# Running a decoder layer's projections and feed-forward per half of the batch, and pooling the K and V buffers, in a two-layer attention kernel

## The chip, the cores and the metric

The kernel runs on one core of a Trainium2 chip. The metric is the time of one execution on the device in microseconds (us), as the median of several runs. A run counts as slow when it is over 1.5% above the fastest run of the same kernel, else as fast. Ratios are the mean of one kernel's fast runs over the mean of the other's fast runs of the same rounds, with a 95% interval, so they are not quite the ratios of the medians.

## The reference, cut to what matters

```python
B, Sq, D = 4, 1, 512                    # four sequences, one new token each
Hq, Hkv, Sk, Dh = 32, 8, 4096, 128      # GQA: 4 query heads per kv head
F = 1792
# A: q = norm(x) @ wq; softmax(q k^T / sqrt(Dh)) v; @ wo     (k and v: caches, bf16)
# B: (gelu(norm(x) @ w_gate) * (norm(x) @ w_up)) @ w_down
x = x + A(x); x = x + B(x)              # layer 1
x = x + A(x); x = x + B(x)              # layer 2, the same caches and weights
```

There are 32 pairs (batch, kv head). Each has 1 MiB of K and 1 MiB of V, which both layers read: 128 MiB, plus 13.25 MiB of weights, 148 MB in all.

## The kernel before

A layer first works through all 32 pairs' scores, then through all 32 pairs' outputs; projections and the feed-forward part (FFN) follow. Abridged:

```python
K_BUFS = 3; V_BUFS = 3                       # K_j and V_j tiles of 1 MiB
...
for j in range(NPAIR):                       # scores
    K_j = issue_k(j)                         # DMA
    # 32 transposes on TensorE, copied from PSUM to KT_j by VectorE and ScalarE
    # 32 matmuls: sc = KT_j . q
    nc.scalar.activation(out=SCORES[:, j], in_=sc, func=ACT.Copy)
    nc.vector.tensor_reduce(out=colmax, in_=sc, op=ALU.max)            # 3 buffers
    nc.gpsimd.partition_all_reduce(gmax, colmax, P, RED.max)           # 3 buffers
    nc.gpsimd.tensor_scalar(out=NEGB[:, j], in0=gmax, scalar1=-scale, op0=ALU.mult)
for j in range(NPAIR):                       # outputs
    V_j = ...                                # DMA
    # 4 x pexp = exp(scale * SCORES + NEGB), with SUMS, on ScalarE      (4 buffers)
    nc.gpsimd.partition_all_reduce(den, SUMS[:, j], P, RED.add)
    # 32 matmuls: ot += V_j . pexp           (2 PSUM buffers)
    nc.vector.tensor_tensor(out=OT_bf[:, b, qsl], in0=ot, in1=1/den, op=ALU.mult)
# out-proj (128 matmuls), layer norm, FFN (3 x 56), layer norm, next q-proj (128)
```

A scheduler places the instructions of the two loops on each engine ahead of time, so the first outputs are woven into the last scores. PSUM is where the kernel puts the tiles that TensorE writes (tp, sc, ot); a denominator is the sum that a softmax divides by.

Of the kernel before, what the change touches and what calls it, by code (L numbers as in the profile page):

```python
# [15 lines left out]
P = 128  # L16

K_BUFS = 3
KT_BUFS = 3
V_BUFS = 3  # L20
# [8 lines left out]
def kernel(  # L29
# [27 lines left out]
    KB = KD * B  # L57
    assert Hq * B <= P and B <= P and rep <= P and KB <= 512
    assert C * rep * 4 <= 2048, "scores tile must fit a PSUM bank"
    assert 2 * KF * B * 4 <= 2048 and rep * B <= C * rep  # L60
# [11 lines left out]
    kin = ctx.enter_context(tc.tile_pool(name="kin", bufs=K_BUFS))  # L72
    ktp = ctx.enter_context(tc.tile_pool(name="ktp", bufs=KT_BUFS))
    vin = ctx.enter_context(tc.tile_pool(name="vin", bufs=V_BUFS))
# [38 lines left out]
    H_bf = state.tile([P, KF, B], BF16, name="H_bf")  # L113
# [4 lines left out]
    def layer_norm_T():  # L118
        xs = small.tile([P, 2, KD, B], FP32, name="xs", tag="xs")
        nc.vector.tensor_tensor(out=xs[:, 1], in0=XT[:], in1=XT[:], op=ALU.mult)  # L120
        st = ps_misc.tile([P, 2, KD, B], FP32, name="st", tag="misc")
        nc.tensor.matmul(st[:, 0], lhsT=ones_f[:, :], rhs=XT[:, :, :], start=True, stop=True)
        nc.tensor.matmul(st[:, 1], lhsT=ones_f[:, :], rhs=xs[:, 1], start=True, stop=True)
        sums = small.tile([P, 2, B], FP32, name="sums", tag="sums")
        nc.vector.tensor_reduce(out=sums[:], in_=st.rearrange("p s k b -> p s b k"),
                                axis=AX.X, op=ALU.add)
        negmean = small.tile([P, B], FP32, name="negmean", tag="negmean")
        nc.vector.tensor_scalar(out=negmean[:, :], in0=sums[:, 0, :], scalar1=-1.0 / D,
                                scalar2=None, op0=ALU.mult)
        msq = small.tile([P, B], FP32, name="msq", tag="msq")  # L130
        nc.vector.tensor_tensor(out=msq[:, :], in0=negmean[:, :], in1=negmean[:, :],
                                op=ALU.mult)
        var = small.tile([P, B], FP32, name="var", tag="var")
# [3 lines left out]
        hv = small.tile([P, B], I32, name="hv", tag="hv")  # L137
        nc.vector.tensor_single_scalar(out=hv[:, :], in_=var[:, :].bitcast(I32), scalar=1,
                                       op=ALU.arith_shift_right)
        rstd = small.tile([P, B], FP32, name="rstd", tag="rstd")  # L140
        nc.vector.tensor_tensor(out=rstd[:, :].bitcast(I32), in0=magic[:, :], in1=hv[:, :],
                                op=ALU.subtract)
        r2 = small.tile([P, B], FP32, name="r2", tag="r2")
        for _it in range(2):
# [5 lines left out]
        xc = small.tile([P, KD, B], FP32, name="xc", tag="xc")  # L150
        nc.vector.tensor_tensor(out=xc[:], in0=XT[:],
                                in1=negmean[:, :].unsqueeze(1).broadcast_to([P, KD, B]),
                                op=ALU.add)
        nc.vector.tensor_tensor(out=xnT_bf[:], in0=xc[:],  # L154
                                in1=rstd[:, :].unsqueeze(1).broadcast_to([P, KD, B]),
                                op=ALU.mult)

    def add_yT_to_XT(yT_ps):
        nc.vector.tensor_tensor(out=XT[:], in0=XT[:], in1=yT_ps[:], op=ALU.add)
# [11 lines left out]
    def issue_k(j):  # L171
        b, kvh = divmod(j, Hkv)
        K_j = kin.tile([P, C, Dh], BF16, name="K_j", tag="K_j")
        dq.dma_start(out=K_j[:], in_=A_k_cache[b, kvh].rearrange("(p c) d -> p c d", p=P))
        return K_j

    layer_idx = [0]

    def attention_layer():
        first = layer_idx[0] == 0  # L180
        layer_idx[0] += 1
        pre_k = {}
        if first:
            npre = min(K_BUFS, NPAIR)
# [5 lines left out]
        layer_norm_T()  # L190
        for kvh in range(Hkv):
            qps = ps_sc.tile([P, rep, B], FP32, name="qps", tag="sc")
            for h in range(rep):
                m = kvh * rep + h
                for k in range(KD):
                    nc.tensor.matmul(qps[:, h, :], lhsT=wq_sb[:, k, m * Dh:(m + 1) * Dh],  # L196
                                     rhs=xnT_bf[:, k, :], start=(k == 0), stop=(k == KD - 1))
            nc.vector.tensor_copy(out=qT_bf[:, kvh * rep:(kvh + 1) * rep, :], in_=qps[:, :, :])
# [28 lines left out]
        for j in range(NPAIR):  # L227
# [5 lines left out]
            V_j = vin.tile([P, C, Dh], BF16, name="V_j", tag="V_j")  # L233
# [11 lines left out]
            for c in range(C):  # L245
# [3 lines left out]
                                    op=ALU.mult)  # L249

        yT = ps_misc.tile([P, KD, B], FP32, name="yT", tag="misc")
        for dk in range(KD):
            for i in range(Hq):
                nc.tensor.matmul(yT[:, dk, :], lhsT=wo_sb[:, i, dk * P:(dk + 1) * P],  # L254
                                 rhs=OT_bf[:, :, i], start=(i == 0), stop=(i == Hq - 1))
        add_yT_to_XT(yT)

    def ffn_layer():
        layer_norm_T()
        NF = KF * B  # L260
        hg = ps_misc.tile([P, KF, B], FP32, name="hg", tag="misc")
        for m in range(KF):
            for k in range(KD):
                nc.tensor.matmul(hg[:, m, :], lhsT=wg_sb[:, k, m * P:(m + 1) * P],  # L264
                                 rhs=xnT_bf[:, k, :], start=(k == 0), stop=(k == KD - 1))
        g_sb = small.tile([P, NF], FP32, name="g_sb", tag="g_sb")
        nc.vector.tensor_copy(out=g_sb[:, :], in_=hg.rearrange("p m b -> p (m b)"))
        t1 = small.tile([P, NF], FP32, name="t1", tag="t1")
        nc.vector.tensor_tensor(out=t1[:, :], in0=g_sb[:, :], in1=g_sb[:, :], op=ALU.mult)
# [9 lines left out]
        for m in range(KF):  # L279
            for k in range(KD):  # L280
                nc.tensor.matmul(hu[:, m, :], lhsT=wu_sb[:, k, m * P:(m + 1) * P],
                                 rhs=xnT_bf[:, k, :], start=(k == 0), stop=(k == KD - 1))
# [52 lines left out]
```

## Time and profile before

The median was 592.04 us in the first six runs. The profiled run was a slow one. I cut it into stages at marks that the GpSimd and TensorE timelines show: the first max all-reduce; the first all-reduce after the last negation of the layer (from there only V is left); the last 100 matmuls of the out-projection; the first scores of layer 2.

| us | start | layer-1 scores | layer-1 V tail | chain to layer 2 | layer-2 scores | layer-2 V tail | end | span |
|---|---|---|---|---|---|---|---|---|
| before, first profile (slow) | 27.7 | 226.9 | 52.0 | 25.7 | 233.0 | 17.7 | 16.2 | 599.2 |
| before, second profile | 27.3 | 222.2 | 51.1 | 24.8 | 233.9 | 18.2 | 16.2 | 593.7 |

In the profiles PE is TensorE's matmuls, PEld its weight loads, DVE VectorE, ACT ScalarE, POOL GpSimd, and SPq the queue that issues the DMAs. Two rows of slices from the page of the kernel before (40 equal slices of the span, busy tenths), then from its groups of instructions (line, engine, operation, tiles, count; busy us and mean ns of one; idle us just before and what ended it):

```profile
POOL 0001201101010111031100012021101110211100
...
DMA  8968792866496571779977485745675584963560
...
L211 PE MATMUL tp<-ident_bf,K_j 128*128 128x128 bf16 x2048 | 170.3, 254 | 13.9 <-ACT KT_j L169 6.9
...
L223 POOL PARTITION_ALL_REDUCE gmax<-colmax x64 | 23.9, 428 | 225.0 <-issue 153.4
...
L224 POOL TENSOR_SCALAR NEGB<-gmax 128x4 f32<-128x4 f32 x64 | 15.1, 235 | 191.5 <-DVE KT_j L167 115.5
```

GpSimd is busy for 66.4 of 599.2 us (11%), yet its two small operations have 225 and 192 us of idle time before them, and the larger part of the first is "issue": nothing that the profile shows was waited for. The DMA row has two full slices in a row only where V is left alone (270 to 300 us).

### The profile page before, as it was taken

To read this page: it belongs to the slowest core of one execution; us is meant where nothing else is said; L and a number is where in the kernel's file an instruction comes from. 1 tells how busy PE (TensorE), PEld (TensorE's weight loads), DVE (VectorE), ACT (ScalarE), POOL (GpSimd) and SP (SyncE) were. 2 spreads that over 40 slices of the span, in tenths; PEclk is the share of its full clock that TensorE was granted. 3 is DMA by queue.
4 is the path that set the end of the run, shared out by engine and by line. 5 is a ranking of instruction groups with operands and counts; after the bars stand their busy time and mean duration, and the time that the engine had idled before them with its cause. 6 is when DMAs were issued, how large, how long until landed. Compare 5 with 4: busy or idle time off the path is not lost. (4 is left out here: it accounts for less than half of the span.)

```text
span 599.2 us, 16150 instructions
## 1 busy us (share of the span) xinstructions
PE 307.9 (51%) x7016; PEld 295.4 (49%) x7016; DVE 181.8 (30%) x495; ACT 170.9 (29%) x643; POOL 66.4 (11%) x198
## 2 busy tenths in 40 slices
PE   1996834756334410163467993573466436411145
PEld 1986824656334410153466983573466436411144
DVE  2555512534223100031125571442244223100103
ACT  0245411322113430265300244431332225431210
POOL 0001201101010111031100012021101110211100
PEclk9979865887676555565556696865876676555555
DMA  8968792866496571779977485745675584963560
GB/s 334 364 222 288 261 378 97 311 250 256 177 369 232 209 275 80 280 301 378 368 293 276 152 341 220 274 165 207 270 260 209 181 337 159 362 225 114 203 278 2
DMA packets 26551, 149.16 MB, mean 249 GB/s; under 512 B 2152, under 2 KB 8048, under 8 KB 10096
## 3 DMA queue, kind: packets, MB, share of 16 engines
q1 hardware_dynamic: 26480, 148.13, 66.1%
q8 instruction: 55, 0.90, 0.6%
q14 instruction: 16, 0.13, 0.1%
HBM read 148.12 MB, written 0.00 MB: 247 GB/s over the span
## 5 line engine op out<-in xcount | busy, mean ns | idle before, releaser
L211 PE MATMUL tp<-ident_bf,K_j 128*128 128x128 bf16 x2048 | 170.3, 254 | 13.9 <-ACT KT_j L169 6.9
L211 PEld LDWEIGHTS <-K_j 128*128 128x128 bf16 x2048 | 154.0, 116 | 18.6 <-issue 10.8
L167 DVE COPY KT_j<-tp 128x1024 bf16<-128x1024 bf16 x192 | 129.2, 688 | 68.0 <-PE tp L211 60.5
L246 PE MATMUL ot<-pexp,V_j 128*128 128x4 bf16 x2048 | 61.4, 166 | 128.1 <-DVE OT_bf L248 78.8
L216 PE MATMUL sc<-qT_bf,KT_j 128*128 128x4 bf16 x2048 | 63.5, 166 | 121.4 <-DVE colmax L220 120.6
L216 PEld LDWEIGHTS <-KT_j 128*128 128x128 bf16 x2048 | 63.1, 103 | 124.2 <-issue 122.7
L246 PEld LDWEIGHTS <-V_j 128*128 128x128 bf16 x2048 | 58.2, 102 | 131.0 <-issue 82.4
L237 ACT ACTIVATE pexp<-SCORES,NEGB 128x32 bf16<-128x32 f32 x256 | 86.7, 355 | 108.1 <-PE ot L246 101.2
L169 ACT ACTIVATE KT_j<-tp 128x1024 bf16<-128x1024 bf16 x64 | 65.4, 1021 | 108.9 <-PE tp L211 107.3
L218 ACT ACTIVATE SCORES<-sc 128x128 f32<-128x128 f32 x64 | 17.8, 279 | 183.8 <-PE sc L216 183.8
L220 DVE TENSOR_REDUCE colmax<-sc 128x4 f32<-128x128 f32 x64 | 18.4, 289 | 144.5 <-POOL gmax L223 136.1
L223 POOL PARTITION_ALL_REDUCE gmax<-colmax x64 | 23.9, 428 | 225.0 <-issue 153.4
L237 ACT ACTIVATION_READ_ACCUMULATOR pexp<-SCORES,NEGB 128x1 f32 x256 | 48.0, 188 | 0.0
L243 DVE RECIPROCAL rden<-den 128x4 f32<-128x4 f32 x64 | 11.3, 177 | 105.0 <-POOL den L241 102.8
L241 POOL PARTITION_ALL_REDUCE den<-SUMS x64 | 28.5, 481 | 80.7 <-issue 44.1
L224 POOL TENSOR_SCALAR NEGB<-gmax 128x4 f32<-128x4 f32 x64 | 15.1, 235 | 191.5 <-DVE KT_j L167 115.5
L248 DVE TENSOR_TENSOR OT_bf<-ot,rden 128x4 bf16<-128x4 f32 x64 | 10.0, 160 | 63.8 <-PE ot L246 63.2
L196 PEld LDWEIGHTS <-wq_sb 128*128 128x128 bf16 x256 | 7.6, 103 | 6.5 <-issue 6.5
L254 PEld LDWEIGHTS <-wo_sb 128*128 128x128 bf16 x256 | 8.8, 103 | 3.8 <-issue 3.8
L196 PE MATMUL qps<-xnT_bf,wq_sb 128*128 128x4 bf16 x256 | 7.3, 166 | 6.2 <-DVE xnT_bf L154 6.2
L254 PE MATMUL yT<-OT_bf,wo_sb 128*128 128x4 bf16 x256 | 8.8, 168 | 3.0 <-DVE OT_bf L248 3.0
L274 ACT ACTIVATE th<-t_9168 128x56 f32<-128x56 f32 x1 | 0.2, 249 | 20.6 <-DVE t_9168 L272 20.6
(68 smaller groups left out, 51.6 us busy)
## 6 DMA issues: line engine op xcount, KB each, us to landing
K_j<-in_A_k_cache_dram SPq DMA_DIRECT2D x64, 1024.0 KB, 5.7
V_j<-in_A_v_cache_dram SPq DMA_DIRECT2D x64, 1024.0 KB, 7.6
wq_sb<-in_A_wq_dram SPq DMA_DIRECT2D x2, 2048.0 KB, 13.7
wo_sb<-in_A_wo_dram SPq DMA_DIRECT2D x1, 4096.0 KB, 17.9
wg_sb<-in_B_w_gate_dram SPq DMA_DIRECT2D x1, 1792.0 KB
wu_sb<-in_B_w_up_dram SPq DMA_DIRECT2D x1, 1792.0 KB, 10.7
wd_sb<-in_B_w_down_dram SPq DMA_DIRECT2D x1, 1792.0 KB, 10.6
x_bf<-in_A_x_dram SPq DMA_DIRECT2D x1, 4.0 KB
```

Source lines behind the costliest of these rows:

```text
L167: nc.vector.tensor_copy(out=out_ap, in_=in_ap)
L169: nc.scalar.activation(out=out_ap, in_=in_ap, func=ACT.Copy)
L211: nc.tensor.transpose(tp[:, t, :], K_j[:, c, :], ident_bf[:, :])
L216: nc.tensor.matmul(sc[:, c, :], lhsT=KT_j[:, c, :], rhs=qcols, start=True, stop=True)
L218: nc.scalar.activation(out=SCORES[:, j, :, :], in_=sc[:, :, :], func=ACT.Copy)
L220: nc.vector.tensor_reduce(out=colmax[:, :], in_=sc.rearrange("p c h -> p h c"), axis=AX.X, op=ALU.max)
L223: nc.gpsimd.partition_all_reduce(gmax[:, :], colmax[:, :], P, RED.max)
L224: nc.gpsimd.tensor_scalar(out=NEGB[:, j, :], in0=gmax[:, :], scalar1=-scale, scalar2=None, op0=ALU.mult)
L237: nc.scalar.activation(out=pexp[:, :, h], in_=SCORES[:, j, :, h], func=ACT.Exp, bias=NEGB[:, j, h:h + 1], scale=scale, accum_out=SUMS[:, j ...
L241: nc.gpsimd.partition_all_reduce(den[:, :], SUMS[:, j, :], P, RED.add)
L246: nc.tensor.matmul(ot[:, :], lhsT=V_j[:, c, :], rhs=pexp[:, c, :], start=(c == 0), stop=(c == C - 1))
L254: nc.tensor.matmul(yT[:, dk, :], lhsT=wo_sb[:, i, dk * P:(dk + 1) * P], rhs=OT_bf[:, :, i], start=(i == 0), stop=(i == Hq - 1))
```

## The change

The intent was to take layer 1's projections and FFN off the boundary between the layers: once half of the batch has its attention outputs, its out-projection, FFN and layer-2 q-projection run while V of the other half still streams. In the same edit the three K and three V buffers became one pool of six. The diff, cut to its core:

```diff
-K_BUFS = 3
-V_BUFS = 3
+KV_BUFS = 6
...
-        K_j = kin.tile([P, C, Dh], BF16, name="K_j", tag="K_j")
+        K_j = kvin.tile([P, C, Dh], BF16, name="K_j", tag="kv")
...
-            V_j = vin.tile([P, C, Dh], BF16, name="V_j", tag="V_j")
+            V_j = kvin.tile([P, C, Dh], BF16, name="V_j", tag="kv")
...   (layer_norm_T, q_proj, out_proj_add and ffn now take a range b0, nb of the batch)
+            if kvh == Hkv - 1:
+                after_batch(b)
...
+    NBH = (B + 1) // 2
+    def after_batch_l1(b):
+        if b + 1 == NBH or b + 1 == B:
+            b0 = 0 if b + 1 == NBH else NBH
+            nb = b + 1 - b0
+            out_proj_add(b0, nb)
+            ffn(b0, nb)
+            layer_norm_T(b0, nb)
+            q_proj(b0, nb)
```

Layer 2 still does everything for the whole batch at its end.

More of the change, by code (lines that the diff above doesn't have):

```diff
@@ L56 @@
     NPAIR = B * Hkv
-    KB = KD * B
-    assert Hq * B <= P and B <= P and rep <= P and KB <= 512
+    assert Hq * B <= P and B <= P and rep <= P and KD * B <= 256
     assert C * rep * 4 <= 2048, "scores tile must fit a PSUM bank"
-    assert 2 * KF * B * 4 <= 2048 and rep * B <= C * rep
+    assert KF * 4 <= 2048 and 2 * KD * B * 4 <= 2048
     scale = float(Dh) ** -0.5
@@ L71 @@
     pexpp = ctx.enter_context(tc.tile_pool(name="pexpp", bufs=PEXP_BUFS))
-    kin = ctx.enter_context(tc.tile_pool(name="kin", bufs=K_BUFS))
+    kvin = ctx.enter_context(tc.tile_pool(name="kvin", bufs=KV_BUFS))
     ktp = ctx.enter_context(tc.tile_pool(name="ktp", bufs=KT_BUFS))
-    vin = ctx.enter_context(tc.tile_pool(name="vin", bufs=V_BUFS))
     ps_tp = ctx.enter_context(tc.tile_pool(name="ps_tp", bufs=TP_PSUM_BUFS, space=bass.MemoryType.PSUM))
@@ L112 @@
     xnT_bf = state.tile([P, KD, B], BF16, name="xnT_bf")
-    H_bf = state.tile([P, KF, B], BF16, name="H_bf")
     SCORES = state.tile([P, NPAIR, C, rep], FP32, name="SCORES")
@@ L116, with layer_norm_T @@
     SUMS = state.tile([P, NPAIR, rep], FP32, name="SUMS")
-    def layer_norm_T():
-        xs = small.tile([P, 2, KD, B], FP32, name="xs", tag="xs")
-        nc.vector.tensor_tensor(out=xs[:, 1], in0=XT[:], in1=XT[:], op=ALU.mult)
-        st = ps_misc.tile([P, 2, KD, B], FP32, name="st", tag="misc")
-        nc.tensor.matmul(st[:, 0], lhsT=ones_f[:, :], rhs=XT[:, :, :], start=True, stop=True)
-        nc.tensor.matmul(st[:, 1], lhsT=ones_f[:, :], rhs=xs[:, 1], start=True, stop=True)
-        sums = small.tile([P, 2, B], FP32, name="sums", tag="sums")
+    def layer_norm_T(b0, nb):
+        bs = slice(b0, b0 + nb)
+        xs = small.tile([P, KD, nb], FP32, name="xs", tag=f"xs{nb}")
+        nc.vector.tensor_tensor(out=xs[:], in0=XT[:, :, bs], in1=XT[:, :, bs], op=ALU.mult)
+        st = ps_misc.tile([P, 2, KD, nb], FP32, name="st", tag="misc")
+        nc.tensor.matmul(st[:, 0], lhsT=ones_f[:, :], rhs=XT[:, :, bs], start=True, stop=True)
+        nc.tensor.matmul(st[:, 1], lhsT=ones_f[:, :], rhs=xs[:], start=True, stop=True)
+        sums = small.tile([P, 2, nb], FP32, name="sums", tag=f"sums{nb}")
         nc.vector.tensor_reduce(out=sums[:], in_=st.rearrange("p s k b -> p s b k"),
                                 axis=AX.X, op=ALU.add)
-        negmean = small.tile([P, B], FP32, name="negmean", tag="negmean")
+        negmean = small.tile([P, nb], FP32, name="negmean", tag=f"negmean{nb}")
         nc.vector.tensor_scalar(out=negmean[:, :], in0=sums[:, 0, :], scalar1=-1.0 / D,
                                 scalar2=None, op0=ALU.mult)
-        msq = small.tile([P, B], FP32, name="msq", tag="msq")
+        msq = small.tile([P, nb], FP32, name="msq", tag=f"msq{nb}")
         nc.vector.tensor_tensor(out=msq[:, :], in0=negmean[:, :], in1=negmean[:, :],
                                 op=ALU.mult)
-        var = small.tile([P, B], FP32, name="var", tag="var")
+        var = small.tile([P, nb], FP32, name="var", tag=f"var{nb}")
         nc.vector.tensor_scalar(out=var[:, :], in0=sums[:, 1, :], scalar1=1.0 / D,
@@ L136, in layer_norm_T @@
         nc.vector.tensor_tensor(out=var[:, :], in0=var[:, :], in1=msq[:, :], op=ALU.subtract)
-        hv = small.tile([P, B], I32, name="hv", tag="hv")
+        hv = small.tile([P, nb], I32, name="hv", tag=f"hv{nb}")
         nc.vector.tensor_single_scalar(out=hv[:, :], in_=var[:, :].bitcast(I32), scalar=1,
                                        op=ALU.arith_shift_right)
-        rstd = small.tile([P, B], FP32, name="rstd", tag="rstd")
-        nc.vector.tensor_tensor(out=rstd[:, :].bitcast(I32), in0=magic[:, :], in1=hv[:, :],
+        rstd = small.tile([P, nb], FP32, name="rstd", tag=f"rstd{nb}")
+        nc.vector.tensor_tensor(out=rstd[:, :].bitcast(I32), in0=magic[:, :nb], in1=hv[:, :],
                                 op=ALU.subtract)
-        r2 = small.tile([P, B], FP32, name="r2", tag="r2")
+        r2 = small.tile([P, nb], FP32, name="r2", tag=f"r2{nb}")
         for _it in range(2):
@@ L149, in layer_norm_T @@
             nc.vector.tensor_tensor(out=rstd[:, :], in0=rstd[:, :], in1=r2[:, :], op=ALU.mult)
-        xc = small.tile([P, KD, B], FP32, name="xc", tag="xc")
-        nc.vector.tensor_tensor(out=xc[:], in0=XT[:],
-                                in1=negmean[:, :].unsqueeze(1).broadcast_to([P, KD, B]),
+        xc = small.tile([P, KD, nb], FP32, name="xc", tag=f"xc{nb}")
+        nc.vector.tensor_tensor(out=xc[:], in0=XT[:, :, bs],
+                                in1=negmean[:, :].unsqueeze(1).broadcast_to([P, KD, nb]),
@@ L153, in layer_norm_T, with q_proj @@
                                 op=ALU.add)
-        nc.vector.tensor_tensor(out=xnT_bf[:], in0=xc[:],
-                                in1=rstd[:, :].unsqueeze(1).broadcast_to([P, KD, B]),
+        nc.vector.tensor_tensor(out=xnT_bf[:, :, bs], in0=xc[:],
+                                in1=rstd[:, :].unsqueeze(1).broadcast_to([P, KD, nb]),
                                 op=ALU.mult)
-    def add_yT_to_XT(yT_ps):
-        nc.vector.tensor_tensor(out=XT[:], in0=XT[:], in1=yT_ps[:], op=ALU.add)
+    def q_proj(b0, nb):
+        bs = slice(b0, b0 + nb)
+        for kvh in range(Hkv):
+            qps = ps_sc.tile([P, rep, nb], FP32, name="qps", tag="sc")
+            for h in range(rep):
+                m = kvh * rep + h
+                for k in range(KD):
+                    nc.tensor.matmul(qps[:, h, :], lhsT=wq_sb[:, k, m * Dh:(m + 1) * Dh],
+                                     rhs=xnT_bf[:, k, bs], start=(k == 0), stop=(k == KD - 1))
+            nc.vector.tensor_copy(out=qT_bf[:, kvh * rep:(kvh + 1) * rep, bs],
+                                  in_=qps[:, :, :])
@@ new lines, in out_proj_add, with ffn @@
+    def out_proj_add(b0, nb):
+        bs = slice(b0, b0 + nb)
+        yT = ps_misc.tile([P, KD, nb], FP32, name="yT", tag="misc")
+        for dk in range(KD):
+            for i in range(Hq):
+                nc.tensor.matmul(yT[:, dk, :], lhsT=wo_sb[:, i, dk * P:(dk + 1) * P],
+                                 rhs=OT_bf[:, bs, i], start=(i == 0), stop=(i == Hq - 1))
+        nc.vector.tensor_tensor(out=XT[:, :, bs], in0=XT[:, :, bs], in1=yT[:], op=ALU.add)
+    def ffn(b0, nb):
+        bs = slice(b0, b0 + nb)
+        layer_norm_T(b0, nb)
+        NF = KF * nb
+        hg = ps_misc.tile([P, KF, nb], FP32, name="hg", tag="misc")
+        for m in range(KF):
+            for k in range(KD):
+                nc.tensor.matmul(hg[:, m, :], lhsT=wg_sb[:, k, m * P:(m + 1) * P],
+                                 rhs=xnT_bf[:, k, bs], start=(k == 0), stop=(k == KD - 1))
+        g_sb = small.tile([P, NF], FP32, name="g_sb", tag=f"g_sb{nb}")
+        nc.vector.tensor_copy(out=g_sb[:, :], in_=hg.rearrange("p m b -> p (m b)"))
+        t1 = small.tile([P, NF], FP32, name="t1", tag=f"t1{nb}")
+        nc.vector.tensor_tensor(out=t1[:, :], in0=g_sb[:, :], in1=g_sb[:, :], op=ALU.mult)
+        nc.vector.tensor_scalar(out=t1[:, :], in0=t1[:, :], scalar1=0.044715, scalar2=1.0,
+                                op0=ALU.mult, op1=ALU.add)
+        nc.vector.tensor_tensor(out=t1[:, :], in0=t1[:, :], in1=g_sb[:, :], op=ALU.mult)
+        th = small.tile([P, NF], FP32, name="th", tag=f"th{nb}")
+        nc.scalar.activation(out=th[:, :], in_=t1[:, :], func=ACT.Tanh, scale=GELU_C)
+        nc.vector.tensor_scalar(out=th[:, :], in0=th[:, :], scalar1=0.5, scalar2=0.5,
+                                op0=ALU.mult, op1=ALU.add)
+        nc.vector.tensor_tensor(out=th[:, :], in0=th[:, :], in1=g_sb[:, :], op=ALU.mult)
+        hu = ps_sc.tile([P, KF, nb], FP32, name="hu", tag="sc")
+        for m in range(KF):
+            for k in range(KD):
+                nc.tensor.matmul(hu[:, m, :], lhsT=wu_sb[:, k, m * P:(m + 1) * P],
+                                 rhs=xnT_bf[:, k, bs], start=(k == 0), stop=(k == KD - 1))
+        H_bf = small.tile([P, KF, nb], BF16, name="H_bf", tag=f"H_bf{nb}")
+        nc.vector.tensor_tensor(out=H_bf.rearrange("p m b -> p (m b)"), in0=th[:, :],
+                                in1=hu.rearrange("p m b -> p (m b)"), op=ALU.mult)
+        yT = ps_misc.tile([P, KD, nb], FP32, name="yT2", tag="misc")
+        for dk in range(KD):
+            for k in range(KF):
+                nc.tensor.matmul(yT[:, dk, :], lhsT=wd_sb[:, k, dk * P:(dk + 1) * P],
+                                 rhs=H_bf[:, k, :], start=(k == 0), stop=(k == KF - 1))
+        nc.vector.tensor_tensor(out=XT[:, :, bs], in0=XT[:, :, bs], in1=yT[:], op=ALU.add)
@@ L172, in issue_k, with attention_layer @@
         b, kvh = divmod(j, Hkv)
-        K_j = kin.tile([P, C, Dh], BF16, name="K_j", tag="K_j")
+        K_j = kvin.tile([P, C, Dh], BF16, name="K_j", tag="kv")
         dq.dma_start(out=K_j[:], in_=A_k_cache[b, kvh].rearrange("(p c) d -> p c d", p=P))
         return K_j
-    layer_idx = [0]
-    def attention_layer():
-        first = layer_idx[0] == 0
-        layer_idx[0] += 1
+    def attention_layer(first, after_batch):
         pre_k = {}
         if first:
-            npre = min(K_BUFS, NPAIR)
+            npre = min(3, NPAIR)
             halfc = (Hkv + 1) // 2 * rep * Dh
@@ L189, in attention_layer @@
             dq.dma_start(out=wq_sb[:, :, halfc:], in_=wq_dram[:, :, halfc:])
-        layer_norm_T()
-        for kvh in range(Hkv):
-            qps = ps_sc.tile([P, rep, B], FP32, name="qps", tag="sc")
-            for h in range(rep):
-                m = kvh * rep + h
-                for k in range(KD):
-                    nc.tensor.matmul(qps[:, h, :], lhsT=wq_sb[:, k, m * Dh:(m + 1) * Dh],
-                                     rhs=xnT_bf[:, k, :], start=(k == 0), stop=(k == KD - 1))
-            nc.vector.tensor_copy(out=qT_bf[:, kvh * rep:(kvh + 1) * rep, :], in_=qps[:, :, :])
+            layer_norm_T(0, B)
+            q_proj(0, B)
         for j in range(NPAIR):
@@ L249, in attention_layer @@
                                     op=ALU.mult)
-        yT = ps_misc.tile([P, KD, B], FP32, name="yT", tag="misc")
-        for dk in range(KD):
-            for i in range(Hq):
-                nc.tensor.matmul(yT[:, dk, :], lhsT=wo_sb[:, i, dk * P:(dk + 1) * P],
-                                 rhs=OT_bf[:, :, i], start=(i == 0), stop=(i == Hq - 1))
-        add_yT_to_XT(yT)
-    def ffn_layer():
-        layer_norm_T()
-        NF = KF * B
-        hg = ps_misc.tile([P, KF, B], FP32, name="hg", tag="misc")
-        for m in range(KF):
-            for k in range(KD):
-                nc.tensor.matmul(hg[:, m, :], lhsT=wg_sb[:, k, m * P:(m + 1) * P],
-                                 rhs=xnT_bf[:, k, :], start=(k == 0), stop=(k == KD - 1))
-        g_sb = small.tile([P, NF], FP32, name="g_sb", tag="g_sb")
-        nc.vector.tensor_copy(out=g_sb[:, :], in_=hg.rearrange("p m b -> p (m b)"))
-        t1 = small.tile([P, NF], FP32, name="t1", tag="t1")
-        nc.vector.tensor_tensor(out=t1[:, :], in0=g_sb[:, :], in1=g_sb[:, :], op=ALU.mult)
-        nc.vector.tensor_scalar(out=t1[:, :], in0=t1[:, :], scalar1=0.044715, scalar2=1.0,
-                                op0=ALU.mult, op1=ALU.add)
-        nc.vector.tensor_tensor(out=t1[:, :], in0=t1[:, :], in1=g_sb[:, :], op=ALU.mult)
-        th = small.tile([P, NF], FP32, name="th", tag="th")
-        nc.scalar.activation(out=th[:, :], in_=t1[:, :], func=ACT.Tanh, scale=GELU_C)
-        nc.vector.tensor_scalar(out=th[:, :], in0=th[:, :], scalar1=0.5, scalar2=0.5,
-                                op0=ALU.mult, op1=ALU.add)
-        nc.vector.tensor_tensor(out=th[:, :], in0=th[:, :], in1=g_sb[:, :], op=ALU.mult)
-        hu = ps_sc.tile([P, KF, B], FP32, name="hu", tag="sc")
-        for m in range(KF):
-            for k in range(KD):
-                nc.tensor.matmul(hu[:, m, :], lhsT=wu_sb[:, k, m * P:(m + 1) * P],
-                                 rhs=xnT_bf[:, k, :], start=(k == 0), stop=(k == KD - 1))
-        nc.vector.tensor_tensor(out=H_bf.rearrange("p m b -> p (m b)"), in0=th[:, :],
-                                in1=hu.rearrange("p m b -> p (m b)"), op=ALU.mult)
-        yT = ps_misc.tile([P, KD, B], FP32, name="yT2", tag="misc")
-        for dk in range(KD):
-            for k in range(KF):
-                nc.tensor.matmul(yT[:, dk, :], lhsT=wd_sb[:, k, dk * P:(dk + 1) * P],
-                                 rhs=H_bf[:, k, :], start=(k == 0), stop=(k == KF - 1))
-        add_yT_to_XT(yT)
@@ L292, with after_batch_l2 @@
-    attention_layer()
-    ffn_layer()
-    attention_layer()
-    ffn_layer()
+            if kvh == Hkv - 1:
[7 more added lines that the diff above has]
+            ffn(b0, nb)
+            layer_norm_T(b0, nb)
+            q_proj(b0, nb)
+    def after_batch_l2(b):
+        if b + 1 == B:
+            out_proj_add(0, B)
+            ffn(0, B)
@@ L297 @@
+    attention_layer(True, after_batch_l1)
+    attention_layer(False, after_batch_l2)
     xoT = state.tile([P, KD, B], BF16, name="xoT")
```

## The prediction

In it a switch is the change from one of GpSimd's two operations to the other, to which it puts both gaps of a round; what the first half's chain holds for 22 us in the first rival is TensorE.

> **What bounds the kernel now.** I read the engine shares first: no engine is above 51% and the DMA engines are at 66%, so nothing is simply full. Then the chain of waits: its largest part is "issue", time in which an engine waited for nothing that the profile shows. In order of time that issue time sits on GpSimd, so I read the GpSimd timeline, and then windows over its gaps.
>
> The page's chain, then two rounds of the layer-2 scores phase in that chain in order of time, then the GpSimd timeline over two rounds (start, busy time, operation, idle time before it in brackets):
>
> ```profile
> issue 19%; PE 12%; DMA 4%; DVE 3%; POOL 3%; ACT 1%; POOLq 0%; ACTq 0%; DVEq 0%
> ...
> 402.74 10.35 issue
> 413.09 0.40 POOL gmax L223
> ...
> 423.62 9.31 issue
> ```
>
> ```profile
> 391.59 1.11 POOL L223 PARTITION_ALL_REDUCE gmax<-colmax  x3 [10.09 <-issue]
> 392.61 1.34 POOL L241 PARTITION_ALL_REDUCE den<-SUMS  x3
> 401.53 0.86 POOL L224 TENSOR_SCALAR NEGB<-gmax 128x4 f32<-128x4 f32 x3 [7.59 <-DVE KT_j L167]
> 413.09 1.10 POOL L223 PARTITION_ALL_REDUCE gmax<-colmax  x3 [10.70 <-issue]
> ```
>
> GpSimd works in rounds of three (batch, kv head) pairs: three max all-reduces, some denominator all-reduces, a gap, three negations, a gap. The work is 2 to 3 us, the two gaps 17 to 18 us. In the program's order an extra GpSimd instruction stands at each switch between the all-reduce and the plain negation, and the negation has no semaphore wait except on GpSimd itself, so I do not believe the named releaser (DVE). [...] Since colmax and gmax have three buffers, everything upstream (transposes, K loads) moves at this pace.
>
> Next, windows over gaps and stages (stretch, length, busy time and count per engine, granted clock, DMA share, GB/s):
>
> ```profile
> 92.46:98.40 5.94, 0.00 (x0) 0.00 (x0) 0.00 (x0) 0.00 (x0) 0.01 (x2) 0.50 0.03 10
> 107.31:116.74 9.43, 5.74 (x91) 5.10 (x89) 5.72 (x9) 3.31 (x4) 0.00 (x0) 0.97 0.93 348
> 402.39:413.09 10.70, 1.39 (x26) 1.27 (x23) 0.34 (x2) 1.45 (x8) 0.00 (x1) 0.68 0.89 349
> 543.16:549.08 5.92, 0.00 (x0) 0.00 (x0) 0.00 (x0) 0.00 (x0) 0.00 (x0) 0.50 0.01 6
> 254.56:306.57 52.01, 24.16 (x668) 22.02 (x669) 8.87 (x45) 22.43 (x121) 8.98 (x21) 0.53 0.91 354
> 306.57:332.28 25.71, 21.19 (x493) 20.63 (x492) 11.85 (x58) 2.19 (x3) 0.00 (x0) 0.57 0.60 229
> 371.54:472.80 101.26, 56.56 (x1184) 55.40 (x1184) 36.40 (x78) 30.87 (x102) 13.20 (x41) 0.70 0.63 230
> 565.29:583.00 17.71, 8.01 (x252) 7.45 (x253) 2.91 (x18) 4.11 (x24) 3.81 (x9) 0.50 0.60 239
> ```
>
> Read the first four as one experiment: a switch takes 5.9 us when the data DMA is idle and 9.4 to 10.7 when it runs near 350 GB/s. Bytes moved during a switch thus cost time: (10.7 - 5.9) us over 349 GB/s x 10.7 us = 3.7 MB, about 1.3 us per MB (estimate).
>
> The last four are the stages that the change touches: the layer-1 tail of V (52.0 us, DMA-bound: 0.91 share), the chain from the last output of attention to the first layer-2 scores (25.7 us), five scores rounds of layer 2 (20.25 us each), and the layer-2 tail of V (17.7 us). The profiled run was slow (601 against a median of 592.04), which I carry as a 1.5% scale on differences and otherwise ignore.
>
> [...] the trace shows the stretch, not the cause. [...] 100 out-proj matmuls with only four moving columns take 2.81 us, the same 28 ns spacing as their weight loads (99 in 2.72 us). So half a batch costs as much TensorE time as a whole one.
>
> **The change part by part.**
>
> Splitting layer 1's projections and FFN adds a second pass over the weights: 128 (out-proj) + 3 x 56 (FFN) + 128 (q-proj) = 424 pairs of weight load and matmul, x 28 ns = 12 us of TensorE, plus two layer norms of about 4.3 us DVE latency. TensorE is not the bound in the V tail, but the order matters: the built order puts the first half's chain in the tail, with only four pairs' V matmuls woven into it.
>
> The boundary chain of the second half stays: out-proj, layer norm, FFN, layer norm, q-proj, 424 weight loads as before. It covers half the columns, but its 25.7 us are weight loads and fixed-cost small DVE operations. Extra K copies land in the second norm, three x 0.69 us, and fewer in the first: +1 us. The intended gain, a shorter boundary, is thus nearly zero.
>
> The shared pool of six turns the DMA order into pure K, V, K, V (the built SP order has 32 K, 32 V, 32 K, 32 V; before, V loads of layer 2 were woven between the K loads). The GpSimd order changes with it. In layer 1 it is the same as before. In layer 2, before: 23 denominators ahead of the tail and 9 in it; after: 16 ahead and 16 in it, with five rounds that hold no denominator and during which only K is loaded.
>
> Layer-1 scores: up to three more MB are loaded before the tail starts, weights come later in one burst; about +1 us net.
>
> Layer-1 tail: at its start 13 V are released, so 16 have been issued with three buffers and 19 with six. 13 remain, not 16: at 2.8 us each (16 V in about 48 us) that alone is -8.5 us. Against it stands the first half's chain: from the last V that the first half needs (V15, about 4.5 us into the tail) out-proj to FFN end is 12.8 us by the final chain of the trace (583.00 to 595.8), the norm and q-proj 8 us, four woven pairs partly in the gaps: until about 27 us into the tail. By then only V up to V24 or V25 can be issued, since slots are freed by TensorE; from there six loads x 2.7 us + 5 us for the first + 1.2 us end at 49 us. So -3 us, not -8.5.
>
> Layer-2 scores: five rounds lose their V loads and ten denominators (x 0.42 us = 4 us). K-only rounds in layer 1 ran 16.1, 18.3 and 18.1 us (starts 82.26, 98.40, 116.74; 178.38, 196.47), mean 17.5. 5 x (20.25 - 17.5) = -14. The first two rounds lose one or two V loads, -1; the later ones get V in bursts, +3. Sum -12.
>
> Layer-2 tail: before, 28 V had been issued at its start and four were left; after, 16 + 2 released + 6 slots = 24, so eight are left. Four more x 2.5 us (landing spacing at the end of the trace) = +10. The final chain (16 us) is unchanged.
>
> Sum: +1 - 3 + 1 - 12 + 10 = -3 us. 592 - 3 = 589; I say 588 for the more favourable early rounds.
>
> **The rivals.**
>
> First, real pipelining pays: if the scheduler's woven pairs fill the first half's gaps and the DMA never stops, the layer-1 tail gives its full -8.5, and if the layer-2 rounds fall to 16.5 us the scores give -18. The time would be near 576. For it: six slots are 16 us of buffer. Against it: [...] the first half's chain holds it for some 22 us.
>
> Second, the bytes are just moved: 148 MB have to come in, and V loads taken out of the rounds return in the tail at 2.5 to 2.8 us each, more than their 1.3 us in a round. If the rounds shrink less (17.5 reached only sometimes, say 19 us) the gain there is 6 us, and the time is 595 to 600. For it: the gaps before the max all-reduce are already full of K traffic in layer 1 (9.43 us at 348 GB/s).
>
> Third, a new wait: V slots come from K tiles, so a late transpose delays V, a denominator waits and GpSimd with it; 605 or more. Against it: by the order, V0 is issued a round before its denominator's successor is needed.
>
> **Range and chances.** The five terms err independently by about 2, 5, 2, 5 and 3 us: root of the squares 8 us. Predicted 588 us, 577 to 599 eight times in ten. Faster by over 2% means below 580.2: 0.19. Slower by over 2%, above 603.9: 0.07. Within 2%: 0.74.
>
> **What would show it.** GpSimd rounds in the middle of layer 2 at 17 to 18 us with no denominators: right; still 20: the contention step is wrong. The tail of layer 2 near 27 us with 16 denominators at its start, right; below 20, the slot count is wrong. The layer-1 tail 47 to 52 us with a hole in the DMA share while the first half runs: right; 44 us without a hole: the first rival. The chain after the last layer-1 output near 26 us. If this chain shrinks by more than 5 us, my claim that half a batch costs a whole one is wrong.

## The result, and the profile after

The changed kernel took 602.45 us (median of 10 runs, 595.11 to 606.85) against 594.51 (20 runs): 1.0094 of before, interval 1.005 to 1.0138. Run again with more rounds it took 600.81 against 595.28: 1.0104, 1.0054 to 1.0153. So it is 1% slower, clear of noise but within 2%, and outside my range.

The stages, in two profiles of each kernel. The first two rows are slow runs, the next two come from one chip (the changed kernel's a fast run, the other a single run whose 595.6 us lies among that chip's fast runs):

| us | start | layer-1 scores | layer-1 V tail | chain | layer-2 scores | layer-2 V tail | end | span |
|---|---|---|---|---|---|---|---|---|
| before, 1st | 27.7 | 226.9 | 52.0 | 25.7 | 233.0 | 17.7 | 16.2 | 599.2 |
| changed, 1st | 27.7 | 234.4 | 49.3 | 26.1 | 224.2 | 27.9 | 16.2 | 605.8 |
| before, 2nd | 27.3 | 222.2 | 51.1 | 24.8 | 233.9 | 18.2 | 16.2 | 593.7 |
| changed, 2nd | 27.6 | 228.6 | 50.0 | 26.7 | 224.7 | 27.8 | 16.2 | 601.7 |
| difference, 1st and 2nd | 0, +0.3 | +7.5, +6.4 | -2.7, -1.1 | +0.4, +1.9 | -8.8, -9.2 | +10.2, +9.6 | 0, 0 | +6.6, +8.0 |
| predicted | 0 | +1 | -3 | +1 | -12 | +10 | 0 | -3 |

Both signs of the layer-2 exchange are as predicted: V loads leave the scores and come back in the tail. The GpSimd timeline of the changed kernel (second profile), two middle rounds of layer 2, now without denominators (the first of the five middle rounds still has three):

```profile
406.75 1.10 POOL L263 PARTITION_ALL_REDUCE gmax<-colmax  x3 [8.56 <-issue]
414.73 0.85 POOL L264 TENSOR_SCALAR NEGB<-gmax 128x4 f32<-128x4 f32 x3 [6.88 <-issue]
424.64 1.10 POOL L263 PARTITION_ALL_REDUCE gmax<-colmax  x3 [9.06 <-issue]
433.07 0.85 POOL L264 TENSOR_SCALAR NEGB<-gmax 128x4 f32<-128x4 f32 x3 [7.33 <-issue]
444.13 1.11 POOL L263 PARTITION_ALL_REDUCE gmax<-colmax  x3 [10.21 <-issue]
```

Windows of the same profile: the first round of layer 1, the five middle rounds of layer 2, and three pieces of the layer-1 tail (its start, which holds the first half's out-projection; the rest of the first half's chain; what follows it). Columns as in the prediction's windows:

```profile
27.60:48.70 21.10, 16.45 (x286) 15.60 (x283) 9.64 (x16) 7.83 (x18) 0.65 (x3) 0.78 0.94 363
...
370.30:462.30 92.00, 53.36 (x960) 51.61 (x960) 34.42 (x62) 18.55 (x30) 10.24 (x34) 0.69 0.47 172
...
256.24:268.00 11.76, 7.50 (x248) 7.45 (x248) 4.69 (x32) 5.56 (x32) 4.22 (x10) 0.50 0.67 231
268.00:286.00 18.00, 14.23 (x492) 14.09 (x493) 6.83 (x45) 5.99 (x34) 1.29 (x3) 0.50 0.66 243
286.00:305.00 19.00, 9.65 (x292) 8.72 (x290) 2.54 (x17) 9.65 (x57) 3.44 (x8) 0.50 1.00 402
```

and the windows of the kernel before (second profile) that answer to the first two:

```profile
27.32:43.22 15.90, 15.25 (x269) 14.68 (x267) 9.01 (x16) 6.69 (x17) 0.65 (x2) 0.72 0.70 255
...
365.45:465.43 99.98, 56.82 (x1184) 55.88 (x1184) 36.34 (x78) 30.87 (x102) 13.14 (x40) 0.70 0.63 232
```

Three things are to be seen. The five middle rounds fell from 20.0 to 18.4 us each, with the DMA share down from 0.63 to 0.47: freed bandwidth that nobody uses, because GpSimd still sets the pace. In the layer-1 tail the DMA share is 0.66 to 0.67 while the first half's chain runs, and 1.00 at 402 GB/s once it is over: the hole is there. And the first round of layer 1 grew from 15.9 to 21.1 us, with more data moving in it. The order of DMA issues suggests why; from the kernel before, then from the changed one (start, length of the run of issues, tile, count; the first row was asked for up to 60 us only, in both kernels 16 K are issued before wo):

```profile
19.84 38.52 SPq L174 DMA_DIRECT2D K_j<-in_A_k_cache_dram  x11
...
68.65 0.43 SPq L204 DMA_DIRECT2D wo_sb<-in_A_wo_dram  x1
```

```profile
3.75 53.76 SPq L225 DMA_DIRECT2D K_j<-in_A_k_cache_dram  x13
57.57 0.43 SPq L244 DMA_DIRECT2D wo_sb<-in_A_wo_dram  x1
```

With six slots the fourth K is issued at 3.75 instead of 19.84 us, and wo 11 us earlier. The FFN weights come later instead (from 151.29 us in one burst, before at 127.56, 147.00 and 166.46).

### The profile page after: what moved, and what is told of

Read it like the earlier page. It is cut to its first block, busy times and chain, and to the rows that moved or that the text cites.

```text
span 605.8 us, 17105 instructions
## 1 busy us (share of the span) xinstructions
PE 323.4 (53%) x7448; PEld 312.2 (52%) x7448; DVE 189.5 (31%) x548; ACT 169.9 (28%) x644; POOL 66.2 (11%) x198
## 5 line engine op out<-in xcount | busy, mean ns | idle before, releaser
L251 PE MATMUL tp<-ident_bf,K_j 128*128 128x128 bf16 x2048 | 172.5, 257 | 9.8 <-ACT KT_j L220 7.8
L251 PEld LDWEIGHTS <-K_j 128*128 128x128 bf16 x2048 | 157.9, 118 | 14.2 <-issue 13.2
L258 ACT ACTIVATE SCORES<-sc 128x128 f32<-128x128 f32 x64 | 17.8, 279 | 184.5 <-PE sc L256 184.5
L172 PEld LDWEIGHTS <-wo_sb 128*128 128x128 bf16 x384 | 13.0, 103 | 7.4 <-issue 7.3
L172 PE MATMUL yT<-OT_bf,wo_sb 128*128 128x2 bf16 (+1 forms) x384 | 12.9, 166 | 6.4 <-DVE OT_bf L288 6.3
L162 PEld LDWEIGHTS <-wq_sb 128*128 128x128 bf16 x384 | 10.9, 100 | 8.1 <-issue 8.1
L162 PE MATMUL qps<-xnT_bf,wq_sb 128*128 128x2 bf16 (+1 forms) x384 | 10.9, 164 | 7.7 <-DVE xnT_bf L151 7.6
L183 PE MATMUL hg<-xnT_bf,wg_sb 128*128 128x2 bf16 (+1 forms) x168 | 4.8, 165 | 6.8 <-DVE xnT_bf L151 6.8
## 6 DMA issues: line engine op xcount, KB each, us to landing
wo_sb<-in_A_wo_dram SPq DMA_DIRECT2D x1, 4096.0 KB, 18.2
```

Source lines behind the costliest of these rows:

```text
L162: nc.tensor.matmul(qps[:, h, :], lhsT=wq_sb[:, k, m * Dh:(m + 1) * Dh], rhs=xnT_bf[:, k, bs], start=(k == 0), stop=(k == KD - 1))
L172: nc.tensor.matmul(yT[:, dk, :], lhsT=wo_sb[:, i, dk * P:(dk + 1) * P], rhs=OT_bf[:, bs, i], start=(i == 0), stop=(i == Hq - 1))
L251: nc.tensor.transpose(tp[:, t, :], K_j[:, c, :], ident_bf[:, :])
```

## The experiments

My theory after the result (A): the switches between GpSimd's two operations pace the scores, since they last longer beside DMA traffic; the pool moves DMA traffic between those rounds and the tails and is by itself about neutral; the split costs in the tail, because TensorE is held while V slots are full. Rivals: (B) all loss comes from the pool; (C) the split pays and the pool eats it; (D) the rounds are not bound by the switches at all. Letters E to G stand for rivals that single runs were to settle.

### One part alone: split only, pool only

Split only: the changed kernel with the old buffers.

```diff
-KV_BUFS = 6
+K_BUFS = 3
+V_BUFS = 3
```

> The changed kernel with the old buffers (three for K, three for V), so only the split into batch halves is left. Theory A ([...] the split itself costs only in the layer-1 tail): layer-1 scores as before (226.9 us from first to last round), layer-1 tail 57 to 60 us instead of 52.0, since three slots leave the DMA idle while the first half runs; chain after it near 26; layer 2 as before within 4 us. Time about 1.0% over before. Theory B (all of the loss comes from the pool): time equal to before within 0.4%, tail at 52. Theory C (the split pays and the pool eats the gain): time below before by 1%.

Pool only: the changed kernel with one "half" that holds the whole batch, run twice on different chips.

```diff
-    NBH = (B + 1) // 2
+    NBH = B
```

> The changed kernel with one half that holds the whole batch, so only the shared pool of six is left. Theory A: layer-1 scores +7 us as in the changed kernel (234.4), layer-1 tail 43 to 45 us (no first half in it), layer-2 scores -9 us, layer-2 tail +10 us (27.9); sum near 0, time within 0.5% of before. Theory B: about 1% over before, as the changed kernel. Theory C: more than 1% over before.

> The pool-only kernel once more, to see whether pool and split add up. First time 0.985 of before. Additive with the changed kernel at 1.010 and the split at 1.0165: 0.985 to 0.994. First two rounds of layer 1 38 to 43 us (before: 34), all of layer-1 scores 225 to 229 us, layer-1 tail with chain 68 us, layer-2 scores 222, layer-2 tail with the end 44 us.

| kernel | median us, before beside it | ratio, interval | layer-1 scores | layer-1 V tail | layer-2 scores | layer-2 V tail |
|---|---|---|---|---|---|---|
| split only | 608.16, 596.14 | 1.0165, 1.0105 to 1.0226 | 225.3 | 62.5 | 235.0 | 17.8 |
| pool only | 588.76, 596.14 | 0.9851, 0.9804 to 0.9898 | 225.0 | 40.0 | 224.1 | 27.7 |
| pool only again | 586.62, 594.04 | 0.9901, 0.9867 to 0.9936 | 227.8 | 40.1 | 222.9 | 27.6 |
| both (changed, again) | 600.81, 595.28 | 1.0104, 1.0054 to 1.0153 | 228.6 | 50.0 | 224.7 | 27.8 |

(The profile of split only was a slow run; each stage is one profile. On the chip of the second pool-only run one run of before at 583.57 us set the bar so low that 8 of 29 counted as fast; by the medians the ratio would be 0.9875.)

B and C fall: the pool gains 1.0 to 1.5%, the split costs 1.65% alone and 2 to 2.6% on top of the pool. My theory A had the signs but was too mild: it expected the pool neutral within 0.5% and the split to cost 1.0%. In the tail the two show cleanly. The split adds 10 to 11 us with three slots (51.1 and 52.0 to 62.5) and 10 us with six (40.0 to 50.0). The windows over the whole tail, split only, pool only, and both (the changed kernel, second profile):

```profile
252.82:315.27 62.45, 36.50 (x1088) 34.80 (x1089) 16.29 (x98) 22.44 (x122) 8.95 (x21) 0.50 0.77 291
```

```profile
252.76:292.75 39.99, 20.35 (x637) 18.74 (x638) 6.41 (x42) 20.85 (x120) 8.95 (x21) 0.50 0.92 376
```

```profile
256.24:306.20 49.96, 32.33 (x1056) 31.15 (x1057) 14.22 (x95) 21.21 (x121) 8.95 (x21) 0.50 0.80 305
```

With six slots the same 15 MB (length times GB/s) go through at 376 GB/s without the split and at 305 with it; with three slots 18 MB go through at 354 (before) or 291. TensorE is not full over the tail (36.5 of 62.5 us busy, 32.3 of 50.0), though it is busy for 14.2 of 18.0 us of the window that holds most of the chain. That it lacks freedom to run the V matmuls that release the slots, more than time, is my reading; where the chain stands is tested below.

A second reading came unasked. Up to the layer-1 tail the pool-only kernel and the changed one have the same instructions in the same order on every engine (the traces agree in this), yet their layer-1 scores took 225.0, 227.8, 228.6 and 234.4 us. A single profile's 7 us in this stage is therefore not all the change's.

### Both kernels again, and a shallower K prefetch

> The kernel before, once more, for a profile on the same chip as the next two. The pool-only kernel and the changed kernel have the same instructions in the same order on every engine until the layer-1 tail, yet their profiled layer-1 scores took 225.0 us (fast run) and 234.4 us (slow run). So part of the +7.5 us that the first comparison showed there may be the run and not the change. Expect layer-1 scores within 3 us of 226.9.

> The changed kernel, once more, on the same chip. Theory A (pool -1.5%, split +1.65%, nearly additive): time within 0.0 to 0.9% over before; layer-1 scores 225 to 229 us in a fast profile; tail 49 to 50; layer-2 scores 9 to 11 us shorter than before; layer-2 tail 10 us longer. Rival E (pool and split interact in the layer-1 scores): 233 us or more there again.

> The changed kernel, but K of layer 1 may use only three of the six buffers; V and all of layer 2 use six. Theory A [...]: the first two rounds fall from 38 to 42 us back to 34, layer-1 scores 3 to 5 us shorter, time 0.5 to 0.8% below the changed kernel. Rival F (the same bytes pass anyway, so what the first rounds lose later rounds gain): layer-1 scores and time equal within 0.3%.

The edit of the last: two tags of three buffers each; the first 32 tiles (K of layer 1) use one of them, everything later alternates.

```diff
-        K_j = kvin.tile([P, C, Dh], BF16, name="K_j", tag="kv")
+        K_j = kvin.tile([P, C, Dh], BF16, name="K_j", tag=kv_tag(True))   # V_j alike
+    def kv_tag(is_k):
+        n = kv_ctr[0]; kv_ctr[0] += 1
+        if n < NPAIR: return "kva"
+        return "kvb" if n % 2 == 0 else "kva"
```

And the same on the pool-only kernel:

> The pool-only kernel with K of layer 1 held to three of the six buffers. If the early deep prefetch costs the 5 to 8 us that the first two rounds lose: first two rounds 32 to 35 us instead of 38 to 42, time 0.7 to 1.2% below the pool-only kernel, so 0.975 to 0.983 of before. If later rounds take it back: 0.985 to 0.990 as the pool-only kernel.

The first two rounds fell to 32.5 and 32.7 us (before: 34.1 and 34.3; with six slots for K: 38.5 to 43.2), and layer-1 scores to 223.6 and 222.9 us. But the time did not follow: 601.01 us (1.0116) against 600.81 for the changed kernel, and 587.4 us (0.9849, 0.9789 to 0.9909) against 588.76 and 586.62 for pool only. In the profile of the first, layer 2 took back what layer 1 gained: its scores took 229.3 us against 224.7. So the deep early prefetch does lengthen these two rounds, and a gain from removing it is not shown (rival F has the time right): whatever it is, it stays inside these intervals, some 0.5%.

### The negation off GpSimd

> The kernel before with the negation on the vector engine, so GpSimd runs only all-reduces [...]. [...] (theory A): the 48 gaps of 6 to 12 us vanish, a round of three pairs falls from 20 us to some 12 us (TensorE), time 410 to 450 us. If the rounds are bound by the chain through TensorE, evacuation and max (rival D): within 3% of before.

> The changed kernel with the negation on the vector engine. Theory A: 400 to 450 us like its counterpart. [...] the change should now be neutral to 3% faster than the same edit of the kernel before (the six slots cover the hand-overs). Rival D: near the changed kernel, 600 us.

> Only the shared pool, with the negation on the vector engine [...]. The changed kernel with this edit took 420.9 us, the kernel before with it 458.5. If the pool gives this 8% (DMA always has a free slot): 415 to 422 us. If the split gives it: 450 to 458 us.

> The split with the old buffers and the negation on the vector engine: the fourth corner beside 458.5 (neither), 413.8 (pool), 420.9 us (both). If the split costs by itself, because it holds TensorE while three slots run dry: 463 to 472 us. If the split gains something [...]: below 456.

The edit is one word in each of the four kernels:

```diff
-            nc.gpsimd.tensor_scalar(out=NEGB[:, j, :], in0=gmax[:, :], scalar1=-scale,
+            nc.vector.tensor_scalar(out=NEGB[:, j, :], in0=gmax[:, :], scalar1=-scale,
```

| us (ratio to before) | three and three buffers | pool of six |
|---|---|---|
| no split | 458.51 (0.768) | 413.77 (0.696) |
| split | 465.86 (0.786) | 420.88 (0.705) |

The order of switches is gone and with it 23% of the time: rival D falls. The packed trace names the switch: the kernel before has 100 MODIFY_POOL_CONFIG instructions on GpSimd, four at the start and two at each of the 48 changes between the two operations; with this edit only the four at the start are left. The 48 switches took 401.9 us of the 599.2 us span in the first profile (5.9 to 12.0 us each); they went when 64 negations of 0.23 us on GpSimd became 64 of 0.17 us on VectorE. From the page of the kernel before with this edit, the DMA row and the chain that ended last:

```profile
DMA  8977999899999999999994837999999999999930
...
DMA 40%; PE 28%; ACT 12%; DVE 10%; issue 6%; SPq 3%; POOL 0%; ACTq 0%; POOLq 0%; DVEq 0%
```

"issue", 19% before, is 6%, GpSimd is off the chain, and the DMA has taken its place. With the pool it is full; windows of the pool-only kernel with this edit, a stretch of scores and one that runs into V:

```profile
40.00:160.00 120.00, 91.16 (x2104) 85.39 (x2101) 64.55 (x159) 52.12 (x154) 15.15 (x39) 0.84 1.02 398
110.00:200.00 90.00, 42.51 (x1214) 39.05 (x1212) 19.30 (x79) 45.81 (x233) 13.87 (x33) 0.58 1.02 414
```

In this world the pool is worth 9.8% (458.5 to 413.8), presumably since a K or V load can use any free slot (my reading; no run tests it apart); the split still costs 1.6 to 1.7% by the medians (about 2% for three buffers, if each is taken against before in its own job). My expectation for the changed kernel, neutral to 3% faster than its counterpart, was too small: it was 8% faster, all of it the pool's. Pool only with the negation on VectorE beats both kernels by 30%.

### Where the first part's chain stands

```diff
-    NBH = (B + 1) // 2
+    NBH = 1
```

> The changed kernel with the first part cut after one batch instead of two, so that its chain of projections and FFN starts about 18 us earlier, [...] where TensorE idles and V slots are full anyway. Theory A (the split costs where it stands: it holds TensorE in the DMA-bound tail): tail with chain falls from 78 to 70-73 us, time 590 to 596, below the changed kernel by 0.8% or more. Rival G (the split costs because of its 12 us of added TensorE work, wherever it stands): as the changed kernel, 600 us.

It took 591.31 us (median of 22 runs, before beside it 594.04; ratio of fast runs 1.0003, 0.9955 to 1.0052, with the low bar told above). Its profile, a slow run, shows a layer-1 tail of 41.4 us, nearly that of pool only, because the first part's FFN ended at 237 us, some 20 us before the tail began. The same added TensorE work (424 weight loads) thus adds 1.3 us to the tail from there, and 10 us when it stands in the tail: rival G, which expected 600 us, falls. But it is not free: in the same job pool only took 586.62 us, 4.7 less. So half to two thirds of the split's cost (by fast runs or by medians) went with the place of the chain. The rest lies in no single stage of this profile (layer-1 scores 230.1 against 227.8, layer-2 scores 224.5 against 222.9, tail 41.4 against 40.1) and stays open. Nor is there a gain to set against it, since the chain after the tail stays: 26.8 us with three batches in it, 25.7 and 26.3 us with four in the pool-only kernels.

### What stretches a switch

> The kernel before with half a MB of useless load per pair in layer 1 only (29 x 0.52 = 15 MB into a tile that nothing reads). Theory A, at 1.3 us per MB [...]: the twelve layer-1 rounds grow from a mean of 18.6 to 18.9 us to about 20.5, layer-1 scores +15 to +20 us, the rounds of layer 2 unchanged. Rival D (the rounds' length does not come from DMA traffic; the DMA has over 25% idle time in them): layer-1 rounds within 0.5 us of before.

```diff
             K_j = pre_k.pop(j) if j in pre_k else issue_k(j)
+            if first and j >= 3:
+                junk = junkp.tile([P, C // 2, Dh], BF16, name="junk", tag="junk")
+                dq.dma_start(out=junk[:], in_=A_k_cache[b, kvh].rearrange(...)[:, :C // 2, :])
```

The single run took 617.88 us (before beside it 594.04), but layer-1 scores took 218.5 us, not 240: the opposite sign. The loss came after them, since tail and chain took 102.8 us instead of 77.7 and 75.9. The experiment was also a poor one. The scheduler answered the extra loads by moving V work out of these rounds (28 denominators were left for after them, against 21 before), so that the data moved during the 24 layer-1 switches rose only from 51.1 to 54.8 MB (sums of GB/s times length over the gaps). The switches' sum was 196.0 us, against 201.3 and 196.8 in the two profiles of before. The few more bytes did not lengthen them; a fixed price per MB for every switch does not hold, and some switches with 262 to 271 GB/s beside them took only 6.1 and 6.3 us.

> The kernel before, whose layer 1 works on its first three K and V tiles again and again: the result is wrong on purpose, the instructions of the engines are of the same kinds, but after the weights (about 60 us) layer 1 moves no data. [...] (what is left of theory A after the extra-load run): gaps near 5.9 us in nearly every layer-1 round after the weights, rounds of 14 to 15 us instead of 18 to 21. If the length comes from something else (engines' work[...]): rounds of 18 us and more. Layer 2 is the control: 20 us a round.

```diff
-            K_j = pre_k.pop(j) if j in pre_k else issue_k(j)
+            K_j = pre_k[j % K_BUFS] if first else issue_k(j)      # V_j alike, from three tiles
```

Its output is wrong, which doesn't matter for the time. The comparison's tolerance let it pass all the same. The single run took 515.18 us. The GpSimd timeline of three layer-1 rounds without traffic, and the window over the first of them:

```profile
109.22 1.10 POOL L225 PARTITION_ALL_REDUCE gmax<-colmax  x3 [6.00 <-issue]
110.23 1.33 POOL L247 PARTITION_ALL_REDUCE den<-SUMS  x3
118.46 0.85 POOL L226 TENSOR_SCALAR NEGB<-gmax 128x4 f32<-128x4 f32 x3 [6.90 <-issue]
125.23 1.10 POOL L225 PARTITION_ALL_REDUCE gmax<-colmax  x3 [5.92 <-issue]
```

```profile
109.22:125.23 16.01, 13.92 (x288) 13.45 (x288) 7.59 (x18) 7.68 (x30) 3.04 (x9) 0.68 0.01 3
```

So traffic does stretch the switches: 16 us a round instead of 20 in layer 2 of the same run, with more denominators in the round, not fewer. And the two directions differ. The switch to the all-reduce takes 5.9 to 6.3 us in quiet rounds and about 9 to 10 in busy ones. The switch to the negation takes 6.6 to 7.4 us with nothing moving, and 7 to 8 in the usual rounds of before, so most of its length was never traffic. My expected 14 to 15 us missed both this and the three denominators. Over layer 1, the 24 switches fell from 201.3 us with 51.1 MB beside them to 162.5 us with 17.2 MB (this run's sums: 84.9 us to the negation and 77.6 us to the all-reduce): 38.8 us for 33.9 MB, 1.1 us per MB on average, though not per switch.

The twelve profiles of kernels that still switch say more (288 switches of each kind; means by the GB/s that ran beside them, worked out from the packed traces):

| us, beside | under 20 GB/s | 20 to 150 | 150 to 250 | 250 to 320 | over 320 |
|---|---|---|---|---|---|
| switch to the all-reduce | 6.0 | 6.3 | 8.4 | 9.2 | 10.0 |
| switch to the negation | 7.0 | 7.1 | 7.2 | 9.0 | 9.1 |

Beside less than 20 GB/s the 36 switches to the all-reduce took 5.84 to 6.44 us and the 12 to the negation 6.6 to 7.4. In the busier classes single switches scatter widely: between 250 and 320 GB/s those to the all-reduce took 6.1 to 11.4 us.

## Why the prediction was wrong

Its mechanism was right in the main. The switches between GpSimd's two operations set the pace (shown by moving the negation: 596.14 to 458.51 us). The chain between the layers did not get shorter for half a batch (25.7 and 24.8 us before, 26.1 and 26.7 after; predicted +1). In the profiles 100 out-projection matmuls take 2.81 us with two moving columns as with four, and the small VectorE operations of a layer norm 0.16 to 0.17 us on half the columns and 0.16 to 0.19 on all. Layer 2 gives up V loads in its scores and pays them back in the tail: predicted +10 for the tail, measured +10.2 and +9.6.

The layer-1 tail came out as predicted in sum (49 us predicted, 49.3 and 50.0 measured), but by luck, from two errors that cancel. Six slots alone gave -11 to -12 us, not -8.5: the windows show 15.0 MB in place of 18.4, which is 9.5 us at the old 354 GB/s, and 376 GB/s for the rest, which is 2.5 more. (The prediction's 2.8 us per load is also not what "16 V in about 48 us" gives, which is 3.0.) And the split took back 10, not 5.5.

Of the miss of 14.5 us (602.45 against 588) 2.5 us is the base: before had 592.04 us in the first six runs and 594.51 in the twenty. Most of the rest comes from two terms that failed, both in the scores. The first is "about +1 us net" for layer-1 scores. It had no working behind it: at the prediction's own 1.3 us per MB, the three more MB that it names are 4 us. Measured were +7.5 and +6.4 us in the two pairs. All five profiles with the six-slot order of layer 1 (225.0, 227.8, 228.6, 230.1 and 234.4) average 229.2 against 224.8 for the three with the old buffers (226.9, 222.2, 225.3): +4.4. The two sets overlap, some of these runs were slow, and the rest lies within the scatter of one program. Nor did the time follow when three slots for K took this loss away, so how much of it reaches the whole time is not shown.

The second is "5 x (20.25 - 17.5) = -14" for the middle rounds of layer 2. The 17.5 us came from three hand-picked rounds of layer 1. One of them, from 178.38 us, loaded V and no K (the last K was issued by 166.4 us), and three rounds between them, which also had no denominator but loaded FFN weights beside K, took 20.4, 21.1 and 20.2 us; all six average 19.0, which would have given -6. The five rounds of layer 2 measured 18.3 and 18.4 us (91.7 and 92.0 us in all), against 20.25 and 20.0 before, so -9.5 and -8.0. Seven denominators left the layer's scores, not ten, and gave 3 of its 9 us: outside the gaps its GpSimd time fell from 30.5 and 30.4 us to 27.5. The switches gave the other 6 (200.5 and 201.4 us before, 194.7 and 195.2 after). The step that failed here is thus the pace of a round without V: 17.5 us in the prediction, 18.3 and 18.4 measured. The reading of four gaps that stood behind it, 5.9 us plus bytes for every gap, mixed two kinds of switch, of which one takes 7.0 us on average with hardly anything moving and 7.2 beside 150 to 250 GB/s. That the first term failed by this reading too is argued, not shown.

With +4.4 and -9 in place of +1 and -12 and the other terms as measured (tail and chain together -2.3 and +0.8, layer-2 tail +10), the sum is about +5 us, and 1% of 595 is 6. The third rival, a denominator that waits for a late V and holds GpSimd, played no part: no round of layer 2 shows it. What stays open is why a single switch takes 6 us in one round and 10 in another beside similar traffic: the queues that the profile lists do not tell. Its instruction queue has 55 packets in the kernel before and the same 55 with the negation on VectorE, so no packet there goes with the 48 switches.

## What to carry to other kernels

Splitting a batch need not split its cost: here 100 out-projection matmuls with their weight loads took 2.81 us with two moving columns as with four. Where such a chain is moved off a boundary, ask what TensorE does there: it added 1.3 us to the tail when it ended before it, and 10 us inside it, where TensorE frees the buffers of a DMA-bound stage. Change one thing at a time: here a pool that gained 1 to 1.5% was hidden under a split that cost 2. And before tuning what overlaps with a bound, ask whether the bound can go: the alternation of two GpSimd operations cost 137.6 us (596.14 to 458.51), and this change moved 5.5 to 8.
